# Mask rows made on chip from nine columns, the first pair's loads issued first, and a new engine and order table: attention, gated convolution and spatial gating on one core

## The chip, the cores and the metric

One core of a Trainium2 chip runs the whole program. The metric is device time in microseconds (us), and lower is better. A run's time is that of the whole execution; the profile's span, from the first to the last instruction, is about two us shorter. A matmul on TensorE (PE in the rows) takes its stationary operand by a weight load (PEld); VectorE is DVE, ScalarE is ACT, GpSimd is POOL, SyncE is SP.

## The reference

Three layers follow one another on B = 4 sequences of S = 576 positions.

```python
scores = scale * np.matmul(q, k.transpose(0, 1, 3, 2))      # 8 heads of 64
mask = block_i >= block_j                                   # blocks of 64 positions
scores = np.where(mask, scores, -1000000000.0)
attn = np.exp(scores - np.max(scores, axis=-1, keepdims=True))
attn = attn / (np.sum(attn, axis=-1, keepdims=True) + 1e-09)
x = np.matmul(attn, v)                                      # heads side by side: 512 wide
...
h = np.maximum(x @ w_in, 0.0)                               # 512 -> 1024
conv_out = sum over k of conv_w[k] * hp[:, k:k + S, :]      # 3 taps along the sequence
x = h * sigmoid(conv_out) @ w_out                           # 1024 -> 512
...
h = np.maximum(x @ w_in, 0.0); u, v = halves of h
v_n = (v - mean) / np.sqrt(var + 1e-06)
out = (u * (w_spatial @ v_n + b_spatial)) @ w_out
```

## The kernel before, in words

The 32 heads are handled as 16 pairs; a pair's two heads lie in the two halves of the 128 partitions. Nearly every float32 product is made of three matmuls on parts: a rounded part (`..._h`, type fp32r) and the rest of it (`..._l`), so each operand is rounded once (a copy to fp32r) and subtracted once. Two weights arrive as 64-bit words and are put together by a few integer operations (`words_to_f32`, `split64`).

A pair goes through these steps. `load_pairs` brings K and Q (`raw`), `prep_pair` rounds them to `kp` and `qp` and the last 64 queries to `qlast` (lines 685, 686 and 666: ACT, DVE or POOL). Five `x` steps on PE find the largest score of each 64-query block: four of them multiply (line 916 in row halves, line 655 for the step with `qlast`, which writes the two `mo` banks or one `st` tile), DVE reduces them (lines 921, 950, 956), `max_up` joins them (line 969), and the fifth transposes the maxima (line 978). They are copied to `mt` and sent by DMA into two rows of `mq` (line 990). The `s` steps multiply K by Q (line 1034 or 1042) and then add mask and maximum in one more product, `mk` by `mq` (line 1046); ACT takes the exponential (line 1055). The `v` step multiplies by V and by ones (line 663), and `norm_a` divides by the sums. Four pairs give a batch's `x`, on which the `m` steps (lines 655 with `x,w1i` and `g,w1o`) do the second layer; each tile of it passes through ACT and DVE (lines 1205 to 1215) and is rounded into `g`. The `p` steps do the third layer.

The mask works through `mk` and `mq`, 128 partitions by 576 columns each. Row 0 (and 64) of `mk` is -1 and meets the maximum in `mq`; rows 1 to 4 of `mk` are 1 in the odd 64-column blocks, and meet rows of `mq` that are -2^30 in the even blocks. Before the change DVE zeroes `mk` and the three `mq` (line 1361), and POOL issues eight DMAs that bring the rows from a constant in memory (line 1332).

The order of all engines is fixed by tables. `SEQ` is a string with one letter for each step of PE (`x`, `y` for the `qlast` step into `mo`, `s`, `v`, `m`, `p`; a capital takes the other ring of PSUM banks; `f` is a filler: `FILL_N` matmuls on a tile of ones, kept for PE to have work). `ORDER` lists for DVE, ACT, POOL and SP which task gives the next instruction, `BIND` which buffer each task takes, and `ENG` which engine does each rounding or subtraction (one letter for each: `K`, `Q` and `QE` are `kp`, `qp` and the two `qlast` parts, `GH` the rounding of `g`). While the program is built, the class `Order` replays a plan of time with a cost for each instruction, and emits the instructions in the tables' order. An engine runs its list strictly in order: an instruction that waits holds all behind it.

At the start, 16 spinning matmuls on the tile of ones (line 1344) keep PE at work until the first loads land. `first` holds SP for `HEAD`; then SP issues the first pair's load in two parts (256 and 320 columns, line 832), with the load of the convolution's weights (`cwr`, line 1377) between them, then pair 1 (line 841) and the rest. A filler before the change writes columns 290 to 512 of both `mo` banks without taking them:

```python
def fill(got):
    o = od_mo[0]
    for _ in range(FILL_N):
        if od.tile:
            for e in range(2):
                r = slice(64 * e, 64 * e + 64)
                nc.tensor.matmul(od_mo[e][:, 290:512], full[r, 0:128], full[r], start=True, stop=True)
```

Of the kernel before, what the change touches and what calls it, by code (L numbers as in the profile page):

```python
# [26 lines left out]
KROWS = 69  # L27
# [1803 lines left out]
```

## Time and profile before

| | us |
|---|---|
| median of 3 runs (lowest, highest) | 598.27 (597.57, 598.81) |
| the profiled execution | 597.48 |
| its span | 595.4 |
| PE busy in the span | 576.0 (97%) |
| DVE busy | 448.4 (75%) |
| ACT busy | 247.6 (42%) |
| POOL busy | 166.0 (28%) |

The sum of any term is made against the profiled execution (597.48, 0.79 under the median). Busy time of PE includes overlapping matmuls counted once. A mean over the span hides that the engines that set the pace change: so the rows further down go by stretches.

### The profile page before, as it was taken

Reading aid. Unit: us, or ns where it says so; the run is one execution under the profiler, and the core shown is the slowest. Engines: PE = TensorE matmul, PEld = TensorE weight load, DVE = VectorE, ACT = ScalarE, POOL = GpSimd, SP = SyncE. Lnnn points to the kernel's source line nnn. Section 1 sums busy time; section 2 is a strip of 40 time slices with the busy share of each in tenths; the row PEclk is TensorE's granted clock in tenths of the full one; section 3 lists DMA queues with packets and bytes.
Section 4 is the critical chain, followed back from the end, with each engine's and each line's share of the span. In section 5 each row is a group of like instructions: output and inputs, shape, how many; then the busy total and the mean of one; then the engine's idle time right before and its main releaser. Section 6 shows DMA issues by size and latency. Waiting matters only on the chain.

```text
span 595.4 us, 11879 instructions
## 1 busy us (share of the span) xinstructions
PE 576.0 (97%) x4606; PEld 514.9 (86%) x4606; DVE 448.4 (75%) x985; ACT 247.6 (42%) x527; POOL 166.0 (28%) x206
## 2 busy tenths in 40 slices
PE   7899998999999999999999999999999999999997
PEld 5666678789988888789988999999899989998997
DVE  6899999988577879858558699866897456456557
ACT  3354666645355525617454565533253023103101
POOL 3346653312233353221500033333311111112121
PEclk9999999999999999999999999999999999999999
DMA  6557542231212334021111736334602500150002
GB/s 188 189 163 229 186 153 94 83 97 68 65 37 84 103 125 144 22 84 61 41 63 58 246 106 193 102 107 138 222 0 90 168 21 0 51 177 14 21 30 91
DMA packets 43542, 61.22 MB, mean 103 GB/s; under 512 B 8949, under 2 KB 34293, under 8 KB 43486
## 3 DMA queue, kind: packets, MB, share of 16 engines
q1 hardware_dynamic: 43226, 60.37, 31.7%
q8 instruction: 36, 0.59, 0.4%
q14 instruction: 20, 0.16, 0.1%
q0 software_dynamic: 256, 0.09, 0.1%
q10 hardware_dynamic: 4, 0.00, 0.0%
HBM read 46.08 MB, written 14.23 MB: 101 GB/s over the span
## 4 chain that ended last, share of the span: by engine, by line
PE 70%; DVE 15%; POOL 4%; ACT 3%; issue 3%; DMA 2%; SPq 0%; DVEq 0%; ACTq 0%; POOLq 0%
PE mo L655 42%; PE s L655 9%; PE st L663 7%; PE st L1042 4%; PE st L1034 2%; PE st L916 2%; DVE cc L1211 2%; PE st L1046 2%; DVE mx L921 1%; DVE w_f L780 1%; DVE g L669 1%; PE st L655 1%; POOL g L666 1%; DMA w_raw<-in_w2o_dram 1%; DMA raw<-in_kq_dram 1%
## 5 line engine op out<-in xcount | busy, mean ns | idle before, releaser
L655 PE MATMUL mo<-x,w1i_h 128*128 128x290 f32 x504 | 106.9, 300 | 0.0
L655 PE MATMUL mo<-g,w1o_h 128*128 128x288 f32 x464 | 98.2, 298 | 0.3 <-DVE y L1248 0.3
L655 PEld LDWEIGHTS mo<-x,w1i_h 128*128 128x128 f32 x504 | 82.8, 188 | 2.0 <-issue 1.3
L655 PEld LDWEIGHTS mo<-g,w1o_h 128*128 128x128 f32 x464 | 76.2, 189 | 3.4 <-issue 2.1
L655 PE MATMUL mo<-x,w1i_l 128*128 128x290 f32 x252 | 75.0, 298 | 0.0
L1211 DVE SCALAR_TENSOR_TENSOR cc<-h,cwt,cc 128x288 f32<-128x288 f32 x128 | 67.1, 539 | 7.6 <-ACT cc L1208 6.6
L655 PE MATMUL mo<-g,w1o_l 128*128 128x288 f32 x232 | 68.5, 295 | 0.0
L1055 ACT ACTIVATE e<-st 128x1024 f32<-128x1024 f32 (+2 forms) x64 | 52.9, 836 | 26.4 <-PE st L1046 24.9
L655 PE MATMUL mo<-x,w2i_h 128*128 128x288 f32 x256 | 52.3, 296 | 0.1
L666 POOL TENSOR_SCALAR g<-ga 128x288 fp32r<-128x288 f32 x40 | 20.2, 512 | 108.8 <-DVE ga L1548 59.7
L921 DVE TENSOR_REDUCE mx<-st 128x2 f32<-128x128 f32 (+2 forms) x64 | 42.4, 680 | 8.5 <-PE st L916 8.5
L655 PEld LDWEIGHTS mo<-x,w1i_l 128*128 128x128 f32 x252 | 47.5, 188 | 0.0
L666 POOL TENSOR_SCALAR g<-cc 128x288 fp32r<-128x288 f32 x23 | 14.9, 651 | 115.8 <-DVE cc L1215 113.0
L663 PE MATMUL st<-e,v 128*64 128x448 f32 (+4 forms) x384 | 46.7, 392 | 0.1
L663 PEld LDWEIGHTS st<-e,v 128*64 128x64 f32 x384 | 25.0, 137 | 22.6 <-issue 16.8
L655 PEld LDWEIGHTS mo<-g,w1o_l 128*128 128x128 f32 x232 | 43.5, 188 | 0.1
L655 PEld LDWEIGHTS mo<-x,w2i_h 128*128 128x128 f32 x256 | 41.4, 188 | 1.0 <-ACT u L1522 0.8
L655 PE MATMUL mo<-ws_h,vnh 128*128 128x288 f32 x135 | 39.6, 297 | 1.1 <-DVE ga L1548 1.1
L655 PE MATMUL s<-w2i_h,x 128*128 128x512 f32 x128 | 39.5, 390 | 0.0
L1046 PE MATMUL st<-mq,mk 64*128 64x320 f32 (+1 forms) x192 | 37.9, 394 | 0.0
L655 PE MATMUL mo<-x,w2i_l 128*128 128x288 f32 x128 | 37.7, 294 | 0.0
L1208 ACT ACTIVATE cc<-h,cwt 128x288 f32<-128x288 f32 x64 | 33.8, 533 | 9.1 <-DVE g L669 8.0
(203 smaller groups left out, 1396.5 us busy)
## 6 DMA issues: line engine op xcount, KB each, us to landing
x2d<-y SPq DMA_DIRECT2D x32, 288.0 KB
x<-x2d SPq DMA_DIRECT2D x16, 576.0 KB
raw<-in_kq_dram SPq DMA_DIRECT2D x15, 576.0 KB
v<-in_vt_dram SPq DMA_DIRECT2D x16, 320.0 KB
rb<-rd SPq DMA_DIRECT2D x32, 144.0 KB
out_dram<-o SPq DMA_DIRECT2D x32, 144.0 KB
x<-in_w2i_dram SPq DMA_DIRECT2D x8, 512.0 KB
w_raw<-in_w1i_dram SPq DMA_DIRECT2D x4, 512.0 KB
```

Source lines behind the costliest of these rows:

```text
L655: nc.tensor.matmul(o, w, x, start=start, stop=stop)
L663: nc.tensor.matmul(o[row:row + m], w, x, start=start, stop=stop)
L666: nc.gpsimd.tensor_scalar(o, i, 1.0, 0.0, ALU.mult, ALU.add)
L669: nc.vector.tensor_tensor(o, a, b, ALU.subtract)
L916: nc.tensor.matmul(st[:, e, o:o + n], qp[r, 128 * c:128 * c + 128], kp[r, 0:n], start=True, stop=True)
L921: return ("DVE", t_dve(2 * i.shape[-1] * (i.shape[2] if len(i.shape) == 4 else 1)), lambda: nc.vector.tensor_reduce(o, i, AX.X, ALU.max), ...
L1034: nc.tensor.matmul(out, keys(RAW[p][:, 0, :], r), RAW[p][r, 1, q0:q0 + nq], start=True, stop=False)
L1042: nc.tensor.matmul(st[:, e, o:o + nq], keys(kx, slice(64 * e, 64 * e + 64)), qx[e], start=j == 0, stop=False)
L1046: nc.tensor.matmul(st[:, e, o:o + nq], keys(mk, r), q[r, q0:q0 + nq], start=False, stop=True)
L1055: yield ("ACT", t_act(2 * n), lambda: nc.scalar.activation(ex[:, :, e0:e0 + n], st[:, :, 0:n], ACTF.Exp, scale=0.125), 0, 0)
L1208: yield ("ACT", t_act(HT, False, 1), lambda: nc.scalar.activation(cc, h[:, o:o + HT], ACTF.Copy, scale=cwt[:, c, 1:2]), 0, P_G)
L1211: yield ("DVE", t_dve(HT, ptr=1), lambda: nc.vector.scalar_tensor_tensor(cc, h[:, o + e:o + e + HT], cwt[:, c, j:j + 1], cc, ALU.mult, ALU ...
```

## The change

- The mask rows are made on chip. One DMA on ACT's queue brings `sel`, nine columns by 128 partitions. ACT makes `mk` in six instructions (`start3`: ones times a column plus a column), POOL makes the first `mq` in four and copies it to the other two (`start`). DVE zeroes only the first `mq`; POOL's eight DMAs are gone. The maxima of any pair now wait for `mqs` as well.
- Both parts of the first pair's load are issued first, then the first block of `w1i`, `cwr`, and pair 1.
- A filler takes one `mo` bank, writes its columns 0 to 222, and gives it back. In a stretch of row-half matmuls it uses 64 rows and one matmul in place of two side by side; `SEQ` has two `f` in place of three.
- The plan counts POOL's roundings on the port that DVE and POOL share, with another cost for them (`t_round`), and a few more DVE instructions. `SEQ`, `ORDER`, `BIND` and `ENG` are new. In all, POOL has 185 listed rows for 206, ACT 556 for 524, DVE 957 for 949: kp and qp roundings on POOL go from 17 to 7, on ACT (whole tiles) from 9 to 17.

```diff
-                for e in range(2):
-                    q.dma_start(out=t[64 * e:64 * e + 5], in_=kc[c])
...
     def start():
-        yield ("POOL", 1.9, consts([(mk, 0)], nc.gpsimd))
+        yield ("wait", ("head",))
+        for c in range(4):
+            yield ("POOL", 0.4 + 0.5 * (c == 0), lambda: nc.gpsimd.tensor_scalar(
+                mq[0][:, 128 * c:128 * c + 64], raw(full[:, 0:64]), sel[:, 5 + c:6 + c], None, ALU.mult), 0, 0, True)
+        for t in mq[1:]:
+            yield ("POOL", t_round(S), lambda: pool_round(t, raw(mq[0])), 0, 0, True)
+        yield ("mark", ("mqs",))
+
+    def start3():
+        yield ("wait", ("head",))
+        for c in range(4):
+            yield ("ACT", 0.25 + 0.5 * (c == 0), lambda: nc.scalar.activation(
+                mk[:, 128 * c + 64:128 * c + 128], raw(full[:, 0:64]), ACTF.Identity, bias=sel[:, 4:5], scale=sel[:, c:c + 1]), 0, 0)
...
+    def fill_step():
+        def fn(got):
+            o = got["mo"][0]
+            for _ in range(FILL_N):
+                mm(o[:, 0:222], full[0:64 if od.tile else 128, 0:128], full[0:64 if od.tile else 128], True, True)
+            slot.append(o)
+        slot = []
+        return dict(needs=[], rings=[("mo", 1)], fn=fn, frees=lambda: [("mo", slot)], tile=od.tile)
...
     def zeros():
-        spin(od_mo[0])
+        nc.scalar.dma_start(out=sel, in_=kc)
+        spin()
         nc.vector.memset(eps, 1e-6)
-        for t in [mk] + mq:
-            nc.vector.memset(raw(t), 0.0)
+        nc.vector.memset(raw(mq[0]), 0.0)
...
-            self.port = start + dur
+            self.port = start + dur - 0.13 * (eng == "POOL")
...
-            return ("POOL", t_round(n), fn, 0, prio, False)
+            return ("POOL", t_round(n), fn, 0, prio, True)
...
-    "K": "APPPPDPPPAAAAPPPP",
+    "K": "DAPADAAPAAPAAAADP",
```

Where the instructions moved, at three places.

SP, the start of its list (`raw` is a pair's K and Q, `w_raw` and `x` hold blocks of `w1i`). Before:

```order
L832 DMA raw<-in_kq_dram 128x2x256
L1377 DMA cwr<-in_cw_dram 128x48
L832 DMA raw<-in_kq_dram 128x2x320
L841 DMA raw<-in_kq_dram 128x1152
L1390 DMA ident<-in_cst_dram 128x128
```

Now:

```order
L830 DMA raw<-in_kq_dram 128x2x256
L830 DMA raw<-in_kq_dram 128x2x320
L790 DMA w_raw_143<-in_w1i_dram 128x4x256
L1384 DMA cwr<-in_cw_dram 128x48
L839 DMA raw<-in_kq_dram 128x1152
L1397 DMA ident<-in_cst_dram 128x128
```

The second part stands next to the first; pair 1 stands behind a block of `w1i`.

PE and DVE around the fillers of pair 1 (the `mo<-kp,qlast` matmuls are its `y` step, `mxl` the reductions of that step, `mo<-full` the fillers). PE before:

```order
L655 MATMUL mo_109<-kp_155,qlast_152 128x288
L655 MATMUL mo_110<-kp_155,qlast_152 128x288
L916 MATMUL st_111<-kp_155,qp_156 128x128 x2
L916 MATMUL st_111<-kp_155,qp_156 128x256 x2
L1352 MATMUL mo_109<-full 128x222
L1352 MATMUL mo_110<-full 128x222
```

PE now:

```order
L653 MATMUL mo_110<-kp_156,qlast_153 128x288
L653 MATMUL mo_111<-kp_156,qlast_153 128x288
L914 MATMUL st_113<-kp_156,qp_157 128x128 x2
L914 MATMUL st_113<-kp_156,qp_157 128x256 x2
L653 MATMUL mo_110<-full 128x222 x2
L1033 MATMUL st_114<-raw 128x256 x2
L653 MATMUL mo_110<-full 128x222 x2
L1045 MATMUL st_112<-mq_149,mk 128x320 x2
```

DVE before:

```order
L969 SCALAR_TENSOR_TENSOR mx<-mxu,lim,mx 128x8
L686 CAST qp_156<-raw 128x576
L778 SCALAR_TENSOR_TENSOR cwr<-cwr 128x24
L686 CAST qlast_152<-raw 64x64
L772 TENSOR_SCALAR w_raw_142<-w_raw_142 128x512
L778 SCALAR_TENSOR_TENSOR w_raw_142<-w_raw_142 128x512
L956 TENSOR_REDUCE mxl<-mo_109 128x1
L956 TENSOR_REDUCE mxl<-mo_110 128x1
```

DVE now:

```order
L967 SCALAR_TENSOR_TENSOR mx<-mxu,lim,mx 128x8
L684 CAST qlast_153<-raw 64x64
L684 CAST qp_157<-raw 128x576
L776 SCALAR_TENSOR_TENSOR w_raw_143<-w_raw_143 128x512
L770 TENSOR_SCALAR cwr<-cwr 128x24
L954 TENSOR_REDUCE mxl<-mo_110 128x1
L778 SCALAR_TENSOR_TENSOR w_f_139<-w_f_139,w_raw_143 128x512
L919 TENSOR_REDUCE mx<-st_113 128x2
L954 TENSOR_REDUCE mxl<-mo_111 128x1
```

The fillers follow the first `mxl` instead of being followed by it, and only one bank is concerned.

POOL at the preparation of pair 14 (`kp`, `qp`, `qlast` in a row). Before:

```order
L666 TENSOR_SCALAR g_119<-cc_133 128x288
L666 TENSOR_SCALAR kp_155<-raw 128x576
L666 TENSOR_SCALAR qp_156<-raw 128x576
L666 TENSOR_SCALAR qlast_152<-raw 64x64
L692 TENSOR_TENSOR x_2817<-xp_131,x_2817 128x576
```

Now, on ACT (and `qp` on DVE, the other half of `qlast` on POOL):

```order
L1054 ACTIVATE e_130<-st_113 128x2x512
L683 ACTIVATE kp_156<-raw 128x576
L1054 ACTIVATE e_130<-st_112 128x2x512
L1212 ACTIVATE cc_134<-cc_134 128x288
L1204 ACTIVATE h_145<-mo_110 128x290
L683 ACTIVATE qlast_153<-raw 64x64
```

Of three instructions in a row on POOL, one is left there.

## Rows read from the trace of the kernel before

**Rows 1.** Windows: busy us of each engine by stage, granted clock, DMA share.

```profile
core 0: us, PE busy (x) PEld busy (x) DVE busy (x) ACT busy (x) POOL busy (x), PEclk, DMA share, GB/s
...
30.00:120.00 90.00, 83.61 (x886) 64.48 (x882) 87.13 (x188) 53.23 (x99) 45.77 (x47) 1.00 0.47 149
120.00:265.00 145.00, 143.15 (x1242) 123.47 (x1243) 112.04 (x231) 68.00 (x139) 43.27 (x47) 1.00 0.27 85
```

**Rows 2.** Chain that ended last, first 26 us: start us, us, what.

```profile
2.09 4.75 DMA raw<-in_kq_dram
...
7.69 0.70 PE st L916 x2
```

**Rows 3.** Timeline of SP: start us, us, line, operation, out<-in.

```profile
0.75 0.66 SPq L832 DMA_DIRECT2D raw<-in_kq_dram  x1
1.47 0.58 SPq L1377 DMA_DIRECT2D cwr<-in_cw_dram  x1
2.09 0.56 SPq L832 DMA_DIRECT2D raw<-in_kq_dram  x1
```

**Rows 4.** Timeline of DVE from 14 us; brackets: idle before, releaser.

```profile
14.43 0.46 DVE L956 TENSOR_REDUCE mxl<-mo 128x1 f32<-128x288 f32 x1 [0.94 <-PE mo L1352]
15.75 0.46 DVE L956 TENSOR_REDUCE mxl<-mo 128x1 f32<-128x288 f32 x1 [0.86 <-PE mo L1352]
```

**Rows 5.** Timeline of PE, 1 to 30 us.

```profile
1.16 3.75 PE L1344 MATMUL mo<-full 128*128 128x222 f32 x16 [1.16 <-DVE eps L1359]
...
15.50 0.72 PE L1046 MATMUL st<-mq,mk 64*128 64x320 f32 x4
17.65 1.12 PE L916 MATMUL st<-kp,qp 64*128 64x384 f32 x4 [1.43 <-DVE mxu L921]
...
20.93 1.42 PE L1034 MATMUL st<-raw 64*128 64x320 f32 x4
...
23.37 0.51 PE L655 MATMUL mo<-kp,qlast 128*128 128x288 f32 x2
...
29.30 0.81 PE L1034 MATMUL st<-raw 64*128 64x320 f32 x4
```

**Rows 6.** Groups by form, DVE: xcount, busy us, mean ns, idle before.

```profile
L1361 DVE MEMSET mq<- 128x576 f32 x3 | 1.6, 538 | 0.2
L669 DVE TENSOR_TENSOR raw<-raw,kp 128x576 fp32r<-128x576 f32 x7 | 5.2, 748 | 1.1 <-PE st L1034 1.0
L669 DVE TENSOR_TENSOR w1o_l<-w_f,w1o_h 128x512 fp32r<-128x512 f32 x7 | 5.9, 845 | 0.0
L686 DVE CAST g<-cc 128x288 fp32r<-128x288 f32 x9 | 2.7, 304 | 0.2
L686 DVE CAST x<-xp 128x576 fp32r<-128x576 f32 x2 | 0.9, 460 | 0.1
```

**Rows 7.** Groups by form, ACT.

```profile
L685 ACT ACTIVATE kp<-raw 128x576 fp32r<-128x576 f32 x4 | 2.7, 672 | 0.0
L685 ACT ACTIVATE w1i_h<-w_f 128x512 fp32r<-128x512 f32 x2 | 1.2, 622 | 1.3 <-DVE w_f L780 1.3
L685 ACT ACTIVATE qlast<-raw 64x64 fp32r<-64x64 f32 x10 | 2.5, 251 | 2.5 <-DMA raw<-in_kq_dram 2.3
```

**Rows 8.** Waits, whole span: engine, line, waited for, us in total, times, longest.

```profile
ACT e L1055 <- PE st L1046: 24.9, 26, 4.6
...
PE st L1042 <- ACT e L1055: 1.2, 2, 0.7
PE st L916 <- ACT e L1055: 0.4, 2, 0.2
PE st L1034 <- ACT e L1055: 0.3, 1, 0.3
```

**Rows 9.** Timeline of POOL and PE, pair 14.

```profile
236.21 2.19 POOL L666 TENSOR_SCALAR qlast<-raw 64x64 fp32r<-64x64 f32 x1
...
238.45 0.53 PE L655 MATMUL st<-kp,qlast 128*128 128x288 f32 x2 [1.12 <-POOL qlast L666]
```

More of the change, by code (lines that the diff above doesn't have):

```diff
@@ L26 @@
 VO = 384
-KROWS = 69
 NQ = 3
@@ L230 @@
     ),
[12 rows of a table removed]
-    ),
     "e0": (
@@ L590, in run, with dma @@
             fn()
-def dma(od, size, fn, prio=0, issue=0.48, hot=False):
+def dma(od, size, fn, prio=0, issue=0.48, hot=False, key=None):
     if size > 65536:
@@ L597, in dma @@
     yield ("SP", issue, fn, 0, prio)
+    if key:
+        yield ("mark", key)
     if hot:
@@ L613, in t_round @@
 def t_round(n):
-    return 0.317 + n * 0.00056
+    return 0.146 + n * 0.00084
 def t_ptt(n):
@@ L702, in attn_moe_moe2_kernel @@
     lim = const.tile([128, 1], F32, name="lim")
+    sel = const.tile([128, 9], F32, name="sel")
     ones = const.tile([128, 32], F32, name="ones")
@@ L745, in bank @@
         return t[:, 0, :] if len(t.shape) == 3 else t
-    od_mo = list(od.slots["mo"])
     full = att.tile([128, 222], F32R, name="full")
@@ L818, in load_pairs @@
     def load_pairs():
-        yield ("wait", ("head",))
         for p in range(NPAIR):
+            yield ("wait", ("head",) if p else ("head0",))
             late = None
@@ L826, in load_pairs @@
             HELD[p] = [slot]
-            od.spawn(prep_pair(p, RAW[p], slot, late), "att")
-            if p == 0:
-                yield ("sleep", 0.01)
+            od.spawn(prep_pair(p, RAW[p], slot, late), "att", 0.0, f"pp{p}")
     def first_load(o, i, part):
-        yield from dma(od, o.shape[1] * o.shape[2] * 512, lambda: nc.sync.dma_start(out=o, in_=i), -1)
+        if part:
+            yield ("wait", ("head1",))
+        yield from dma(od, o.shape[1] * o.shape[2] * 512, lambda: nc.sync.dma_start(out=o, in_=i), -1, key=(("head", "head1")[part == 0],))
         yield ("mark", ("raw", 0, part))
@@ L986, in task @@
                 m = MROW[p] = yield ("take", "mq")
+                yield ("wait", ("mqs",))
                 def row(i, q):
@@ L1290, in head @@
         if c == "f":
-            return dict(needs=[], rings=[], fn=fill, tile=od.tile)
+            return fill_step()
         if c in "xy":
@@ L1325, in attn_moe_moe2_kernel, with ones_by @@
     od.pick = pick
-    def consts(tiles, q):
-        def ld():
-            for t, c in tiles:
-                for e in range(2):
-                    q.dma_start(out=t[64 * e:64 * e + 5], in_=kc[c])
-        return ld
-    def start():
-        yield ("POOL", 1.9, consts([(mk, 0)], nc.gpsimd))
+    def ones_by(n):
+        return raw(full[:, 0:64 * n]).rearrange("p (i x) -> p i x", x=64)
+    def start():
+        yield ("wait", ("head",))
[5 more added lines that the diff above has]
+        yield ("mark", ("mqs",))
@@ new lines, in start3 @@
+    def start3():
[3 more added lines that the diff above has]
+                mk[:, 128 * c + 64:128 * c + 128], raw(full[:, 0:64]), ACTF.Identity, bias=sel[:, 4:5], scale=sel[:, c:c + 1]), 0, 0)
+        even = mk[:, 0:384].rearrange("p (i x) -> p i x", x=128)[:, :, 0:64], mk[:, 384:S].rearrange("p (i x) -> p i x", x=64)[:, 0:3:2, :]
+        for o, n in zip(even, (3, 2)):
+            yield ("ACT", 0.33, lambda: nc.scalar.activation(o, ones_by(n), ACTF.Identity, bias=sel[:, 4:5], scale=0.0), 0, 0)
@@ L1337, in start, with spin @@
         yield ("mark", ("mk",))
-        yield ("POOL", 3.2, consts([(t, 1) for t in mq], nc.gpsimd))
-    def spin(o):
+    def spin():
         nc.vector.memset(raw(full), 1.0)
         for _ in range(SPIN):
-            nc.tensor.matmul(o[:, 290:512], full[:, 0:128], full, start=True, stop=True)
-    def fill(got):
-        o = od_mo[0]
-        for _ in range(FILL_N):
-            if od.tile:
-                for e in range(2):
-                    r = slice(64 * e, 64 * e + 64)
-                    nc.tensor.matmul(od_mo[e][:, 290:512], full[r, 0:128], full[r], start=True, stop=True)
-                od.cost += 0.113
-            else:
-                mm(o[:, 290:512], full[:, 0:128], full, True, True)
+            nc.tensor.matmul(od.slots["mo"][0][:, 0:222], full[:, 0:128], full, start=True, stop=True)
@@ L1484, in task @@
                 if c < 4:
-                    yield ("POOL", t_round(512), lambda: pool_round(vnh[:, c], v), 0, 1)
-                    yield ("DVE", t_dve(512), lambda: sub(vnl[:, c], v, raw(vnh[:, c])), 0, 1)
+                    yield ("POOL", t_round(512), lambda: pool_round(vnh[:, c], v), 0, 1, True)
+                    yield ("DVE", t_dve(512), lambda: sub(vnl[:, c], v, raw(vnh[:, c])), 0, 1, True)
                     yield ("free", "vf", v)
@@ L1494, in task @@
                     ta, tb = vnh[:, 4 + e], vnl[:, 4 + e]
-                    yield ("POOL", t_round(512), lambda: pool_round(ta[own], v[own]), 0, 1)
-                    yield ("DVE", t_dve(512), lambda: sub(ta[far], v[own], raw(ta[own])), 0, 1)
+                    yield ("POOL", t_round(512), lambda: pool_round(ta[own], v[own]), 0, 1, True)
+                    yield ("DVE", t_dve(512), lambda: sub(ta[far], v[own], raw(ta[own])), 0, 1, True)
                     yield ("ACT", t_act(512, False), lambda: nc.scalar.activation(tb[0:64], v[own], ACTF.Copy), 0, 1)
@@ L1594, in parts @@
         else:
-            yield ("POOL", t_round(HT), lambda: pool_round(g[:, 0], src), 0, 1)
+            yield ("POOL", t_round(HT), lambda: pool_round(g[:, 0], src), 0, 1, True)
         yield ("DVE", t_dve(HT), lambda: sub(g[:, 1], src, raw(g[:, 0])), 0, 0, True)
@@ L1709, in ws_unit @@
             yield ("DVE", t_dve(S), lambda: sub(ws_l[96:97, c], r[64:65], raw(ws_l[64:65, c])), 0, 1)
-        yield ("DVE", t_dve(S), lambda: sub(ws_l[0:k, c], r[0:k], raw(ws_h[0:k, c])), 0, 1)
+        yield ("DVE", t_dve(S), lambda: sub(ws_l[0:k, c], r[0:k], raw(ws_h[0:k, c])), 0, 1, True)
         yield ("free", "wr", slot)
@@ L1797 @@
     cst = _np.eye(128, dtype=_np.float32)
-    kc = _np.zeros((2, KROWS - 64, S), dtype=_np.float32)
-    kc[0, 0] = -1.0
-    for c in range(4):
-        kc[0, 1 + c, 128 * c + 64:128 * c + 128] = 1.0
-        kc[1, 1 + c, 128 * c:128 * c + 64] = NEG
+    kc = _np.zeros((128, 9), dtype=_np.float32)
+    for e in (0, 64):
+        kc[e, 4] = -1.0
+        for c in range(4):
+            kc[e + 1 + c, c] = 1.0
+            kc[e + 1 + c, 5 + c] = NEG
     arrs = {
```

75 lines of the change are left out of this document (37 added, 38 removed), and 302 rows, old and new, of tables (BIND, ORDER).

## The prediction

> **What bounds the kernel now.** I read the windows by stage first, since the whole span's 97% for PE says nothing of where time could be won. From 120 to 265 us PE is busy 143.2 of 145 us: there only PE's own work or one of its few waits can give anything. From 30 to 120 us PE is busy 83.6 of 90, but DVE 87.1 of 90, so DVE sets the pace there, with ACT at 53.2 and POOL at 45.8 [rows 1]. What is left is the first 30 us. So I read the chain of waits there: the second part of the first pair's load is issued at 2.09 us and takes 4.75 us to land, and PE can multiply with it at 7.69 [rows 2]. Then the timelines of SP, DVE and PE over that stretch, to see what each of them waits for [rows 3 to 5]. Last, PE's waits, of which the longest late one stands at 238 us [rows 9].
>
> **Part by part.**
>
> Loads. The second part is issued at 2.09 because `cwr` stands ahead of it [rows 3]. In the new list it stands right behind the first, whose issue ends at 0.75 + 0.66 = 1.41; so it goes out at about 1.47, where `cwr` does now: 0.62 earlier. Everything up to the first mask product hangs on it [rows 2]. What moves behind it is pair 1 (past a block of `w1i` and `cwr`); pair 1 is multiplied only after the first pair's maxima (DVE reduces its `qlast` step from 14.43 on [rows 4]), and that is its cover. Without the cover the first exponentials are not touched, only pair 1's. I take **-0.62**; bounds 0 (the transfer is held up by the block behind it) and -0.62.
>
> Fillers. DVE's two reductions of pair 1's `qlast` step each wait for a filler, 0.94 and 0.86 us [rows 4]: the filler writes other columns of the same bank, and stands behind the product and ahead of its reduction. PE then waits 1.43 us for DVE before the next step at 17.65 [rows 5]. In the new order the fillers take the bank after the first reduction has freed it, so DVE waits for no filler. PE can gain at most its own 1.43, as the step ahead, the mask products at 15.50 [rows 5], need their row of maxima by DMA anyway. Against that DVE has one more long instruction (joining a block of `w1i`) between the two reductions. Bounds 0 and -1.43; I take **-1.0**, nearer the wait that the rows show than nothing.
>
> Masks. Three zeroings leave DVE, 3 x 0.538 = 1.6 us [rows 6], but at a time when all wait for the first load: nothing. Eight DMA issues leave POOL. Six instructions come to ACT: four of 64 columns, about 0.25 each by the 64-column rounding, and two longer ones of at most 0.67 each by the 576-column one [rows 7], 2.3 us in all; about as much comes to POOL. Two of ACT's stand ahead of its part of `qp`, 0.5 us, and wait for the nine columns. If these land late, the first product does too, but the gap of PE ahead of the second part at 7.69 [rows 2] takes that up. **0**; bounds 0 and +0.5.
>
> DVE's list. Up to the 17th gate instruction (line 1215, well past the stretch that DVE paces), eight instructions go: two subtractions into `raw` at 0.75, one `w1o_l` at 0.845, five others that I take at the middling 0.46 of an `x` rounding [rows 6], 4.65 in all. Ten come: three `g` roundings at 0.304, two of `x` at 0.46 [rows 6], five others at 0.46, 4.13 in all. Net **-0.5**. Bounds 0 (DVE's waits take it) and -2.1 (with the 1.6 of the zeroings).
>
> ACT's list. Ahead of the first tile of the second layer ACT gets five more `kp` roundings at 0.672, three `w1i_h` at 0.622 [rows 7], and five of like size (0.65): 3.36 + 1.87 + 3.25 = 8.5 us. With 53.2 of 90 us busy [rows 1] that makes about 69%. PE's waits for ACT's exponentials are 1.2 + 0.4 + 0.3 = 1.9 us [rows 8]; raised by 8.5 / 53.2 they grow by **+0.3**. Bounds 0 and, if each of these instructions holds up an exponential that PE waits for, +8.5.
>
> Pair 14. POOL rounds a 64-column piece of `qlast` in 2.19 us where ACT's mean is 0.251, and PE waits 1.12 us for it [rows 7, 9]. In the new lists ACT does `kp`, DVE `qp`, and POOL only one half of `qlast`. That half can be as slow, but comes sooner, with no `kp` and `qp` ahead of it. Bounds -1.12 and 0; I take **-0.7**.
>
> Fillers as work, the plan's port and costs: they change the tables alone, and PE's list is otherwise the same to within six matmuls of 222 columns, four of them side by side with another. 0.
>
> Sum: -0.62 - 1.0 - 0.5 + 0.3 - 0.7 = -2.5. Of the profiled execution, 597.48, that leaves 594.96; the median of the runs shown is 0.79 higher, so the forecast against the median is **595.7 us**.
>
> **A rule weighed: the clock.** The granted clock stands at 1.00 in every window [rows 1], yet the rows say otherwise for the beginning. Four matmuls of 320 columns take 1.42 us at 20.93 and 0.81 at 29.30, and the pair of 288 columns at 23.37 takes 0.51 [rows 5]: before about 23 us PE ran at the lower of its two levels, 1.2 GHz, and rose to 2.4 GHz after having worked without a gap from 17.65 on. The spinning matmuls from 1.16 to 4.91 [rows 5] had not been enough. My sum lets the rise move with the work: it comes earlier by what the work does. The Trainium skill, "TensorE: Matmul & The Clock Gate", section "What's actually happening", says that the array starts throttled, that activity releases it, and that the point of release differs between runs of the same kernel. By that rule the rise need not follow the work, and either half of the dense stretch could go to one level or the other; this is the first rival.
>
> **The rivals.**
>
> *The clock rises elsewhere.* From 17.65 to about 23.4, 5.75 us of PE's work run at half rate and lie on the chain. If the gap of 1.43 us ahead of it closes and the rise comes at the start of it, half is saved: -2.9 more, 592.8 us. For it: PE's work from 13 us on would be without a gap. Against it: the fillers are half the matmuls that they were, and 3.75 us of spinning did not raise it. As far the other way, a rise 5.75 us of work later, it gives 595.7 + 2.9 = 598.6, no change. Chance 0.17 for the early rise.
>
> *The stalls are only traded.* The mask row's DMA, not the filler, decides the product at 15.50, so -1.0 goes; POOL's half of `qlast` at pair 14 is as slow as now, so -0.7 goes; DVE's -0.5 is lost in new waits. What remains is -0.62 + 0.3: 598.27 - 0.3 = 598.0. For it: DVE's list has the same length, and PE is 98% busy after 120 us. With the late clock: chance 0.20.
>
> *ACT's queue becomes what PE waits for.* ACT runs its list strictly in order. The `kp` roundings that it takes over wait for a pair's load, and an exponential stands behind each. Then a score tile is not freed, the next `x` step of PE has no place, and DVE, which paces this stretch, gets nothing to reduce. At the full price of 8.5 in place of 0.3 the time is 595.7 + 8.2 = 603.9. It decides when more than 2.5 + 0.3 + 1.2 = 4.0 us of the 8.5 reach PE, about half. For it: 69% of an in-order engine in a stretch where every engine feeds another. Against it: ACT's exponentials wait 24.9 us for PE, PE 1.9 for them [rows 8]. Chance 0.18.
>
> That the change doesn't do what it says I leave out: the lists show the fillers, loads and masks moved.
>
> **How the numbers follow.** A measurement of this kernel can tell about 0.2%, 1.2 us, from no change (the three runs lie 1.24 apart). The forecast has 0.45, the early clock 0.17, both over 1.2 us faster: 0.62. No change has 0.20, slower 0.18. The range goes from 591.0, the early clock with DVE's larger bound (592.8 - 1.6 = 591.2), up to 599.5, which takes in the traded stalls, the late clock and the beginning of ACT's rival. Below lie some 0.04, above about 0.14 of ACT's 0.18.
>
> **What would show it.** The second part's load issued near 1.5 us and PE's 384-column product near 7.1. No wait of DVE's `mxl` for a filler, and PE's next such product for pair 1 near 16 us in place of 17.65. The pair of 288-column matmuls of pair 2 before 22 us. No wait of PE for POOL's `qlast` over 0.4 us near pair 14. From 30 to 120 us DVE still at 95% or more, with as much of PE's work done some 2 us sooner. I am wrong if PE's waits for ACT's `e` or for ACT's `kp` pass 4 us, if the first product with `kp` comes later than 5.8 us because of the nine columns, or if PE's busy share from 120 to 265 us falls.

## The result, and the profile after

| | before | the change |
|---|---|---|
| median, us (lowest to highest, 4 runs each) | 598.02 (597.57 to 598.81) | 587.22 (586.77 to 587.94) |
| ratio to before, 95% interval | | 0.9819 (0.9802 to 0.9836) |
| the profiled execution, its span | 597.48, 595.4 | 587.56, 585.8 |
| busy: PE, DVE, ACT, POOL | 576.0, 448.4, 247.6, 166.0 | 573.6, 438.0, 260.7, 152.1 |

The change is 10.8 us faster. The forecast was 595.7, 2.3 under the median of this comparison, with a range from 591.0 to 599.5: the sign was right, the size was not, and the measured time lies below the range.

To see where the time came from I took the same matmul in both traces (same operands, same number of its kind) at nine places, and subtracted its times. "Forecast" is the sum of the prediction's terms that belong to a stretch; places are those of the trace after.

| stretch (us of the trace after) | shorter by | forecast |
|---|---|---|
| 0 to 24.9 (head) | 2.24 | 1.62 (loads, fillers) |
| 24.9 to 43.0 | 0.00 | |
| 43.0 to 84.9 | 0.82 | 0.2 (DVE's list, ACT's list) |
| 84.9 to 126.1 | 2.50 | (the same) |
| 126.1 to 199.8 | 0.07 | |
| 199.8 to 242.1 (pair 14) | 1.81 | 0.7 |
| 242.1 to 345.0 | -0.16 | |
| 345.0 to 452.0 (third layer's preparation) | 2.68 | 0 (tables) |
| to the end | -0.02 | |

The sum is 9.94, the difference of the two profiled executions (597.48 - 587.56 = 9.92).

The windows after, which answer to [rows 1] (columns: stretch, its length, busy us and instructions of PE, PE's weight loads, DVE, ACT, POOL, then the granted clock, DMA share, GB/s):

```profile
30.00:120.00 90.00, 85.47 (x904) 67.20 (x901) 84.44 (x197) 58.00 (x108) 34.54 (x32) 1.00 0.47 151
120.00:265.00 145.00, 144.91 (x1278) 126.17 (x1277) 110.83 (x227) 73.42 (x150) 40.99 (x42) 1.00 0.27 86
```

From 30 to 120 us DVE does nine instructions more than before and is busy 2.7 us less; POOL does 15 fewer and is busy 11.2 us less. From 120 to 265 PE is idle for 0.09 us in place of 1.85. The gain from 85 on is plainest in windows of their own, before and after (same columns):

```profile
43.00:85.00 42.00, 38.77 (x471) 28.15 (x471) 40.65 (x91) 24.23 (x38) 24.88 (x22) 1.00 0.64 200
85.00:126.00 41.00, 38.46 (x337) 33.27 (x326) 38.89 (x83) 24.13 (x55) 16.58 (x18) 1.00 0.21 72
```

```profile
43.00:85.00 42.00, 39.51 (x476) 28.79 (x475) 39.33 (x88) 28.39 (x48) 23.37 (x19) 1.00 0.64 197
85.00:126.00 41.00, 40.09 (x345) 35.31 (x344) 38.40 (x89) 25.45 (x54) 8.37 (x10) 1.00 0.22 77
```

From 85 to 126 POOL's time is halved, and DVE does six instructions more in less time.

The head, PE's timeline after (start, us, line, operation; in brackets the idle time before and its releaser), to be held against [rows 5]:

```profile
6.28 1.11 PE L914 MATMUL st<-kp,qp 64*128 64x384 f32 x4 [0.65 <-POOL kp L664]
...
14.88 0.68 PE L914 MATMUL st<-kp,qp 64*128 64x384 f32 x2
...
18.73 1.42 PE L1033 MATMUL st<-raw 64*128 64x320 f32 x4
...
21.11 0.51 PE L653 MATMUL mo<-kp,qlast 128*128 128x288 f32 x2
```

The product with the second part of the load starts at 6.28 (7.69 before), the first product of pair 1 behind the stall at 14.88 (17.65), and the first 288-column pair at 0.51 us, thus at 2.4 GHz, at 21.11 (23.37).

### The profile page after: what moved, and what is told of

Read it like the earlier page. It is cut to its first block, busy times and chain, and to the rows that moved or that the text cites. A ratio compares the mean times of both kernels' runs of the same rounds, so it can differ in the third digit from the quotient of the medians.

```text
span 585.8 us, 11845 instructions
## 1 busy us (share of the span) xinstructions
PE 573.6 (98%) x4600; PEld 514.9 (88%) x4600; DVE 438.0 (75%) x980; ACT 260.7 (45%) x554; POOL 152.1 (26%) x185
## 4 chain that ended last, share of the span: by engine, by line
PE 89%; DVE 6%; DMA 2%; issue 1%; ACT 1%; SPq 0%; DVEq 0%; POOL 0%
PE mo L653 55%; PE s L653 14%; PE st L661 8%; PE st L1041 4%; PE st L1033 2%; PE st L914 2%; PE st L1045 2%; DVE mx L919 1%; PE st L653 1%; DVE w_f L778 1%; DMA rb<-rd 1%; ACT e L1054 1%; DMA raw<-in_kq_dram 1%; DVE xp L1172 1%; DVE mxu L919 0%
## 5 line engine op out<-in xcount | busy, mean ns | idle before, releaser
L1210 DVE SCALAR_TENSOR_TENSOR cc<-h,cwt,cc 128x288 f32<-128x288 f32 x128 | 65.9, 532 | 8.2 <-ACT cc L1207 7.2
L919 DVE TENSOR_REDUCE mx<-st 128x2 f32<-128x128 f32 (+3 forms) x64 | 42.8, 682 | 8.9 <-PE st L914 8.5
L664 POOL TENSOR_SCALAR g<-ga 128x288 fp32r<-128x288 f32 x40 | 18.9, 478 | 114.5 <-DVE ga L1556 54.3
L1212 ACT ACTIVATE cc<-cc 128x288 f32<-128x288 f32 x64 | 27.6, 439 | 23.1 <-DVE cc L1210 22.9
L1204 ACT ACTIVATE h<-mo 128x290 f32<-128x290 f32 x63 | 25.7, 409 | 23.6 <-PE mo L653 16.7
## 6 DMA issues: line engine op xcount, KB each, us to landing
x<-x2d SPq DMA_DIRECT2D x16, 576.0 KB
raw<-in_kq_dram SPq DMA_DIRECT2D x15, 576.0 KB
```

The costliest lines, as they stand in the source:

```text
L664: nc.gpsimd.tensor_scalar(o, i, 1.0, 0.0, ALU.mult, ALU.add)
L919: return ("DVE", t_dve(2 * i.shape[-1] * (i.shape[2] if len(i.shape) == 4 else 1)), lambda: nc.vector.tensor_reduce(o, i, AX.X, ALU.max), ...
L1204: yield ("ACT", t_act(290), lambda: nc.scalar.activation(h[:, 1:291], ps[:, 0:290], ACTF.Relu), 0, 0)
L1210: yield ("DVE", t_dve(HT, ptr=1), lambda: nc.vector.scalar_tensor_tensor(cc, h[:, o + e:o + e + HT], cwt[:, c, j:j + 1], cc, ALU.mult, ALU ...
L1212: yield ("ACT", t_act(HT, False), lambda: nc.scalar.activation(cc, cc, ACTF.Tanh, scale=0.5), 0, P_G)
```

## The experiments

Each run's arrivals at the same places, against the trace of the change or of before, in us (plus is later or longer). "Time" is a median where more than one run was timed; e5, e6, e7, e10, e11, e13, e14 and e18 were timed once. These runs were made on four other chips, on which the kernel before has medians from 596.19 to 596.85, so times of different chips are compared by their ratio to before where there is one.

| run | time | to 43 us | 43 to 126 | 200 to 242 | 345 to 452 |
|---|---|---|---|---|---|
| against the change: e1 loads back | 587.79 | +0.18 | +0.21 | 0 | -0.07 |
| e2 old fillers | 587.76 | +0.76 | -0.59 | 0 | -0.04 |
| e3 no fillers | 585.87 | -1.12 | +0.03 | 0 | -0.10 |
| e4 head alone | 595.65 | -1.25 | +5.32 | +1.81 | +2.67 |
| e5 15 roundings | 589.10 | -1.56 | +3.23 | -0.01 | -0.04 |
| e6 30 roundings | 596.73 | -1.54 | +10.70 | 0 | -0.07 |
| e7 15 zeroings | 587.50 | -0.09 | +0.22 | 0 | -0.08 |
| e8 old engines back | 593.19 | -1.14 | +4.81 | -0.01 | -0.07 |
| e10 pair 14 back | 587.27 | -0.88 | +0.52 | +0.12 | -0.04 |
| e12 ten more to ACT | 589.82 | -1.51 | +3.60 | -0.01 | -0.09 |
| e15 the change again | 587.17 | -0.20 | +0.96 | 0 | -0.13 |
| e16 no fillers again | 586.41 | -0.92 | +2.50 | 0 | -0.06 |
| e17 fillers near 70 us | 586.00 | -1.85 | +0.04 | -0.01 | -0.11 |
| e18 old tables from 345 | 592.30 | -0.50 | +0.70 | -0.01 | +4.84 |
| against before: e9 new engines | 599.71 | -1.09 | +4.66 | -0.02 | -0.20 |
| e11 `ga` first | 595.80 | -0.55 | -0.30 | 0 | -0.88 |
| e13 13 to ACT | 594.53 | -0.63 | -1.76 | 0 | -0.31 |
| e14 pair 14 first | 595.71 | -1.04 | +0.09 | -0.74 | +0.05 |

First a caution on the column "to 43 us". e5, e7, e10 and e15 have the same program as the change up to some 35 us, and still differ by up to 1.56 us there; so do the kernels of before (0 to -1.04). TensorE's clock differs there between executions (further down). A difference in the head under 1.5 us between two profiles is therefore no finding by itself. Over several profiles the head's gain stands: the matmul at 24.9 us comes between 25.9 and 27.2 in the five with the head of before, and between 23.5 and 25.0 in seven with that of the change (itself, e5, e6, e7, e10, e15, e18), 1.9 earlier on average.

From 43 to 126 us executions of one program differ as well, with the clock at 1.00: e10, e15 and e18 have the program of the change there and come 0.52, 0.96 and 0.70 later. In e15 the 175 instructions that DVE starts in that stretch take 90.61 us, in the change 89.66; half of the 0.95 is one joining of maxima (`mx<-mxu,lim,mx`) that takes 0.60 us beside a rounding of POOL's and 0.12 without one.

### The head: e1 to e4

e1 puts `cwr` back between the two parts of the first load (here and below, a piece of a table's string).

```diff
-first_load0 first_load1 split64 start2
+first_load0 start2 first_load1 split64
```

> The changed kernel with the convolution's weights loaded between the two parts of the first pair's load again, as before. Theory A (each gain of the first 25 us is kept to the end): the second part is issued some 0.6 us later, the first product of 384 columns comes 0.6 later (6.9 in place of 6.28 us), and the end too: 587.2 + 0.6 = 587.8. Theory B (the stretch that DVE paces swallows what the head gains): the product is 0.6 later, the end is not: 587.2.

The product of 384 columns came at 7.45, 1.17 later (5.66 to 6.28 in the seven profiles with the head of the change), but by 24.9 us only 0.31 was left of it, and the median is 587.79. The order of the loads is worth some tenths of a us; whether 0.3 or 0.6 can't be told here.

e2 lets the fillers write columns 290 to 512 again, without a bank of their own.

> The changed kernel with the fillers of before: they write columns 290 to 512 of both banks without taking them. Theory A: DVE's two reductions of pair 1's last block wait for a filler again (0.9 us each in the profile of before), PE's step with x7, at 14.88 now, comes about 1.4 later, and the end too: 588.6. Theory B: that wait is hidden by the row of maxima, which comes by DMA: x7 and the end are as now, 587.2.

DVE's second reduction waits for a filler again (DVE's timeline of e2):

```profile
14.97 0.46 DVE L953 TENSOR_REDUCE mxl<-mo 128x1 f32<-128x288 f32 x1 [1.34 <-PE mo L1360]
```

Pair 1's product behind it comes at 16.62 in place of 14.88, and 1.2 us are lost by 85 us; from there to 126 us 1.01 come back, and 0.10 is left at the end. What comes back is one instruction of DVE's, the joining of a block of weights. POOL and DVE in the change, then in e2:

```profile
83.27 1.29 POOL L690 TENSOR_TENSOR w1o_l<-w_f,w1o_h 128x512 fp32r<-128x512 f32 x1 [2.42 <-ACT w1o_h L683]
83.32 1.78 DVE L778 SCALAR_TENSOR_TENSOR w_f<-w_f,x 128x512 uint32<-128x512 uint32 x1
```

```profile
84.50 1.81 POOL L689 TENSOR_TENSOR w1o_l<-w_f,w1o_h 128x512 fp32r<-128x512 f32 x1 [2.48 <-ACT w1o_h L682]
84.47 0.69 DVE L777 SCALAR_TENSOR_TENSOR w_f<-w_f,x 128x512 uint32<-128x512 uint32 x1
```

In the change POOL starts 0.05 us earlier and DVE's instruction takes 1.78 us (1.66 to 1.81 in all the other runs made from the change, e4 with its old tables apart); in e2 DVE starts 0.03 earlier and takes 0.69. The wait for the filler was real. How much of it would reach the end without that accident is open: the medians (587.76 and 587.22) don't tell it, as e2's own runs lie 3.7 us apart.

e3 takes the fillers out of `SEQ` altogether.

> The changed kernel without any filler. If the fillers hold up the granted clock, its rise (21 us now) comes later, by up to 5 us of PE's work at half rate: up to 2.5 us more, 589.7. If they are work and nothing else, PE saves four to six matmuls in a stretch where it waits anyway: 587.2, and no more than 0.4 less.

585.87: the fillers don't hold up the clock in the head (the 384-column product of pair 1 stands at 14.96, and 288 columns take 0.54 us from 20.68 on). Its profile is 1.12 us ahead of the change's at 43 us and 1.13 at the end, so a lead from the head isn't always lost in the stretch that DVE paces. How much the fillers cost is taken up with e16.

e4 joins the change's tables up to 22 us to those of before.

> The changed kernel with the tables of the change up to 22 us of the plan and those of before (order, engines, buffers) for all that comes later; masks, loads and fillers as in the change. Theory A: what is gained by 22 us, 2.2 to 2.8 us, is kept and nothing else comes: 598.0 - 2.3 = 595.7. Theory B (swallowed): 598.0. Theory C (an earlier head lets the later lists run as well as they do in the change): 587 to 589.

595.65, ratio 0.9977 (0.9957 to 0.9997). PE is 3.5 us ahead of before at 43 us, and 1.5 at 126. The 2 us are lost by 55 us, and the largest piece is one integer operation of DVE's on `w_raw`: 1.91 us beside a subtraction of POOL's, 0.67 in before. That the old tables always take such a lead back is not shown: e11 and e14, which have them too, are 0.56 and 1.04 ahead at 43 us and 0.85 and 0.95 at 126. About 1 us of the head's gain reaches the end. So the rest, 8 to 9 us, hangs on the tables behind the head.

### Work on POOL: e5 to e9, e12, e13

e5 and e6 add roundings on POOL to the change, which nobody waits for (e6 has `range(2)`); e7 adds zeroings in the same places.

```diff
+    def extra():
+        yield ("wait", ("mk",))
+        for _ in range(1):
+            yield ("POOL", 0.6, lambda: pool_round(dump, raw(mk)), 0, 0, False)
```

> The changed kernel with 15 more roundings of 128x576 on POOL, of the mask into a tile that nobody reads, put into the gaps of POOL's list from 35 to 125 us; POOL's busy time of that stretch is then about that of before (34.5 + 15 x 0.75 = 45.8 us). Theory P (DVE is slowed by POOL's work on SBUF, and DVE sets the pace): DVE's instructions that lie beside POOL's take longer, by 0.2 to 0.25 us for each us of overlap, so 11 us more of POOL cost DVE 2.2 to 2.8 us and PE about as much by 125 us: 589.5 to 590. Theory O (the gain is in the order of the lists alone): POOL is idle two thirds of the time and nobody waits for the extra roundings: 587.2 to 587.6.

> The same with two roundings in each of the 15 gaps, 30 in all. Theory P: twice the price of 15, so 4.4 to 5.6 us: 592. Theory O: up to 1 us, where a pair of them holds up a real one of POOL's: 588.

> 15 zeroings of a 128x576 tile on POOL at the places of the 15 roundings: as much of POOL's time or less, but with one stream (it writes and does not read). If what slows DVE is POOL's reading and writing of SBUF, it costs less than the roundings, about half: 588.4. If it is any work on POOL: as the 15 roundings. If POOL's list itself (the real roundings behind the extra ones start late) is the cause: as the 15 roundings too.

The windows of e5, then of e7:

```profile
30.00:120.00 90.00, 83.96 (x877) 65.94 (x874) 85.42 (x190) 56.73 (x105) 45.70 (x45) 0.98 0.46 146
43.00:85.00 42.00, 39.14 (x463) 29.05 (x460) 38.50 (x84) 26.48 (x46) 25.35 (x25) 0.96 0.62 196
85.00:126.00 41.00, 38.88 (x335) 33.88 (x334) 39.47 (x88) 25.50 (x56) 12.95 (x16) 1.00 0.20 70
```

```profile
30.00:120.00 90.00, 85.41 (x903) 67.06 (x900) 85.43 (x197) 57.88 (x107) 42.27 (x47) 1.00 0.47 151
```

With 15 roundings POOL is as busy as before (45.70; [rows 1] has 45.77), and 3.23 us are lost. Up to 1.7 of them can belong to TensorE's clock, which was granted at 0.65 and 0.78 in two stretches of 3 us ((0.35 + 0.22) x 3). What remains at least, 1.5 us, is 0.1 for each rounding, and alone it would not stand clear of the 0.96 by which e15 differs.

DVE's own rows settle it, as they don't follow that clock: in e16, where it falls to 0.50 (further down), DVE's instructions of the stretch take 89.81 us, in e3, the same program without the fall, 89.66. DVE's list is the same in the change and in e5, e6 and e7, so the 175 instructions that it starts from 43 to 126 us in the change can be compared one by one. They take 89.66 us in the change, 92.94 with 15 roundings on POOL (3.28 more, 0.22 for each), 95.07 with 30 (5.41 more) and 89.65 with 15 zeroings. With 15 zeroings POOL runs as many instructions (47) for nearly as long, and nothing is lost: it isn't POOL's time, and not its list. What differs is that a rounding also reads SBUF. 30 roundings cost PE 10.70, of which up to 5.1 can be stretches at half clock. The Trainium skill, "SBUF — State Buffer", section "SBUF: two separate sides", says that DVE and GpSimd share one pair of ports, that an instruction holds it whole, and that a DVE instruction with two SBUF inputs meets only a GpSimd one that reads SBUF. e5 and e7 agree with that, by 3.28 us against none.

What it does to a DVE instruction stands in the trace of before. DVE's timeline:

```profile
95.09 0.91 DVE L669 TENSOR_TENSOR g<-cc,g 128x288 fp32r<-128x288 f32 x1
...
101.62 0.46 DVE L669 TENSOR_TENSOR g<-cc,g 128x288 fp32r<-128x288 f32 x1
...
102.43 0.46 DVE L1215 SCALAR_TENSOR_TENSOR cc<-cc,h 128x288 f32<-128x288 f32 x1
...
103.83 0.90 DVE L1215 SCALAR_TENSOR_TENSOR cc<-cc,h 128x288 f32<-128x288 f32 x1
```

and POOL's:

```profile
94.83 0.87 POOL L666 TENSOR_SCALAR qp<-raw 128x576 fp32r<-128x576 f32 x1
...
103.57 1.75 POOL L769 TENSOR_SCALAR w_raw<-w_raw 128x512 f32<-128x512 f32 x1
```

The same subtraction takes 0.46 us alone and 0.91 beside POOL's rounding; the same gate product 0.46 alone and 0.90 beside POOL's operation on `w_raw`.

e13 takes load off POOL in the kernel before, and changes nothing else: 13 of its roundings go to ACT, for instance

```diff
-    "K": "APPPPDPPPAAAAPPPP",
+    "K": "APPAPDAPAAAAAPPPP",
```

> The kernel before with 13 roundings of 22 to 125 us moved from POOL to ACT, the same 13 that the change moves from POOL to ACT there, all else as before. Theory P (less work on POOL beside DVE is the gain): at 0.1 to 0.2 us for each rounding taken off, 1.3 to 2.6 us less from 43 to 126 us. Theory O (an engine's list and its places only pay together): no gain there, or a loss of some us, since ACT's list holds exponentials behind roundings that wait for a load.

1.76 us less from 43 to 126 us, 0.135 for each rounding, inside what theory P expected. DVE's list is that of before, and the same 172 instructions take 88.61 us in place of 91.44, 2.83 less or again 0.22 for each rounding. In e11 and e14, where this stretch is as in before, they take 90.71 and 91.61, and PE comes 0.30 earlier and 0.09 later. (The other 0.9 of its 2.65 at the end lie mostly in the head.) So about half of the 3.32 us that the change gains there is had by relieving POOL alone, in the old order. In the change itself, 171 of DVE's instructions of that stretch of before, matched by kind and count, take 88.45 us in place of 90.75.

e8 gives the change the engines of before for 61 instructions of that stretch; e9 gives before the engines of the change for the same 61.

> The changed kernel with the engine of before for each of the 61 roundings, subtractions and copies that the change gave to another engine between 22 and 125 us of the plan; each stands in its new list at the place in time at which it stood in the old one, all else in the order of the change. POOL gets back 14, ACT loses 10, DVE 4. Theory P: DVE's instructions are slowed as before (3.8 us more beside POOL, less some 1.7 for four instructions that leave it), 2 to 4 us lost by 125 us: 589 to 591. Theory O: the order is what gained, and is kept: 587.2 to 588.

> The kernel before, with the engine of the change for each of those 61 roundings, subtractions and copies of 22 to 125 us; each stands in its new list at the place in time at which it stood in the old one, all else (order, head, fillers, masks) as before. Theory P (the choice of engine alone relieves DVE): from 43 to 126 us PE gains the 3.3 us that the change gained there, or somewhat less since the order was not fitted to it: 598.0 - 3 = 595.0. Theory O (engines and order only pay together, since an in-order list needs the places that go with its engines): 597 to 600.

e8 loses 4.81 us from 43 to 126, with the clock at 1.00 throughout, more than the change had gained: with the old engines the order of the change is worse than the old one. e9 loses 4.66, of which up to 3.4 can be half clock from 78 to 87 us; the rest, at least 1.3, is still a loss, and its six runs are slower than before (ratio 1.0048, 1.0031 to 1.0066). So the other half of the gain belongs to the engines and the order together, and neither has it alone. I did not divide it further.

e12 goes on in the same direction: no fillers, and ten more roundings from POOL to ACT.

> The changed kernel without fillers, and with ten more roundings of 30 to 126 us moved from POOL to ACT (five of w1i or w1o, four of kp or qp, one of g), about 9 us of POOL's time. Theory P: at 0.2 to 0.25 us of DVE's time for each us of overlap, 1.8 to 2.2 us less than without fillers alone: 583.9. Rival (ACT's list is the next bound: PE's waits for exponentials, 0.8 and 0.4 us now, grow): 586 to 588.

589.82. POOL is relieved once more, but PE waits more for exponentials: its waits from 43 to 126 us in e12, then in the change (line, what for, us in total, times, longest; one more wait of 0.8 us stands in each):

```profile
PE st L913 <- ACT e L1053: 1.3, 3, 0.5
```

```profile
PE st L914 <- ACT e L1054: 0.4, 2, 0.2
```

The clock fell as well (0.70, 0.50 and 0.66 in three stretches of 3 us from 72 on, up to 3.4 us of the 3.60). DVE's 175 instructions take 89.12 us, 0.54 less than in e3 (89.66), while PE's waits for exponentials in that stretch are 1.1 us longer than there (2.1 and 1.0). So even at full clock a gain is not to be seen. The prediction's third rival, ACT's list, begins to show just beyond the change; its price can't be told from this run, for the clock.

### Pair 14: e10 and e14

e10 puts pair 14's `kp`, `qp` and `qlast` back on POOL, in the change.

> The changed kernel with the preparation of pair 14 on the engines of before: kp, qp and one half of qlast in a row on POOL. If that row is the cause of PE's stop near 238 us of before: POOL's qlast takes about 2 us beside DVE again, PE waits for it 1.1 us or more, and the stretch from 200 to 242 us is 1.4 to 1.8 us longer: 588.6 to 589. If it was the place in POOL's list that delayed it and not the row: no wait of PE, 587.2.

It costs nothing (0.12): POOL's `qlast` takes 0.33 us there. Not the engine, then. In the trace of before POOL stood for 11.69 us in front of a rounding of `g`, with pair 14 behind it:

```profile
232.95 1.13 POOL L666 TENSOR_SCALAR g<-cc 128x288 fp32r<-128x288 f32 x1 [11.69 <-DVE cc L1215]
234.05 0.87 POOL L666 TENSOR_SCALAR kp<-raw 128x576 fp32r<-128x576 f32 x1
```

e14 puts that `g` behind the three, in the kernel before.

```diff
-m52 one1400 one1401 ends14
+one1400 one1401 ends14 m52
```

> The kernel before with pair 14's kp, qp and half of qlast ahead of one rounding of g on POOL and not behind it (POOL stood 11.7 us in front of that g, until DVE had made it). Theory: PE's stop of 1.39 us near 238 us is the place in the list: it goes, and the stretch from 200 to 242 us is 1.2 to 1.4 us shorter. Rival: DVE keeps POOL's qlast slow, whatever its place (2.19 us for a 64x64 rounding), so PE still waits 0.5 us or more.

POOL in e14:

```profile
231.21 0.81 POOL L666 TENSOR_SCALAR kp<-raw 128x576 fp32r<-128x576 f32 x1 [10.87 <-PE st L1046]
231.98 0.88 POOL L666 TENSOR_SCALAR qp<-raw 128x576 fp32r<-128x576 f32 x1
232.94 0.96 POOL L666 TENSOR_SCALAR qlast<-raw 64x64 fp32r<-64x64 f32 x1
```

PE's wait for `qlast` is gone, and 0.74 of the 1.81 us with it; a new wait of 0.5 us for DVE's `mx` takes part of the place:

```profile
PE st L663 <- DVE mx L950: 0.5, 1, 0.5
```

The place in POOL's list was the cause of the stop, and DVE's list stood close behind it. What else makes up the 1.81 was not tried.

### The third layer's preparation: e11 and e18

In before DVE waits 2.71 us for ACT to make `w_f`, with a product `ga` behind it that PE needs:

```profile
418.25 0.43 DVE L772 TENSOR_SCALAR w_raw<-w_raw 128x512 uint32<-128x512 uint32 x1 [2.71 <-ACT w_f L764]
418.72 0.69 DVE L778 SCALAR_TENSOR_TENSOR w_raw<-w_raw 128x512 uint32<-128x512 uint32 x1
419.33 0.45 DVE L1548 TENSOR_TENSOR ga<-u,mo 128x288 f32<-128x288 f32 x1
```

```diff
-p14 w2o_f320*2 p15 w2o_f322
+p14 p15 w2o_f320*2 w2o_f322
```

> The kernel before with one instruction of DVE's list moved: the product ga of the third spatial step stands ahead of the two integer operations on a block of w2o and not behind them (in before DVE waited 2.71 us there for ACT's w_f, with ga ready behind it, and PE then 1.1 us for ga). Theory: PE's wait at 420 us goes, 1.1 to 1.4 us less from 390 to 452 us: 596.8. Rival: the integer operations come later by it, so the weights w2o are late in their turn, and PE waits there instead: 598.

```profile
416.32 0.45 DVE L1548 TENSOR_TENSOR ga<-u,mo 128x288 f32<-128x288 f32 x1 [1.39 <-PE mo L655]
417.19 0.43 DVE L772 TENSOR_SCALAR w_raw<-w_raw 128x512 uint32<-128x512 uint32 x1 [0.42 <-ACT w_f L764]
```

In e11 `ga` is made as soon as PE has its input, DVE's idle time falls to 0.42, and 0.88 us are gained (e9, e13 and e14 differ from before by up to 0.31 in that stretch): a third of what the change gains from 345 to 452 us, by one instruction moved.

> The change with its own tables up to 345 us of the plan and those of before for all that comes later. If the order of the third layer's preparation in those tables is the gain of 345 to 452 us: 2.7 us back, 589.9, with PE's waits near 385, 420 and 447 us of before in their places again. Rival (the gain is that all data are there sooner, whatever the order): 587.2.

592.30: the old tables from 345 us on cost 2.17 us from 390 to 452, what the change had gained there (2.12), and 2.67 from 345 to 390, where the change had gained 0.56; the rest of that is a wait of 1.9 us for DVE's `y` at the place where the two tables are joined. The gain of this stretch is the tables.

### A version that beats both? e15 to e17

> The change itself once more, as a measure for the next kernel on the same chip: 587.2, ratio to before 0.982.

> The change without fillers once more, beside the change on the same chip. If the saving of 1.1 us that its profile showed (all of it by 43 us) is no accident of the clock: 586.0, 1.0 to 1.4 less than the change. If it is one: the same as the change within 0.4.

The change 587.17, without fillers 586.41, on one chip; the ratios to before are 0.9837 (0.9811 to 0.9864) and 0.9833 (0.9808 to 0.9858). No difference is shown. The profile of e16 takes 2.71 us more from 43 to 85 us than that of e3, which is the same program. Windows of e16, then of e3:

```profile
69.00:72.00 3.00, 1.79 (x19) 1.28 (x19) 2.96 (x9) 1.91 (x4) 1.86 (x2) 0.96 0.29 96
72.00:75.00 3.00, 3.00 (x19) 2.54 (x19) 2.92 (x6) 1.96 (x4) 1.15 (x1) 0.50 0.84 242
75.00:78.00 3.00, 3.00 (x26) 2.78 (x26) 0.03 (x1) 2.16 (x3) 1.31 (x2) 0.50 0.39 141
```

```profile
69.00:72.00 3.00, 1.79 (x20) 1.29 (x17) 2.96 (x9) 2.13 (x4) 1.65 (x2) 1.00 0.32 105
72.00:75.00 3.00, 2.92 (x38) 2.58 (x37) 2.70 (x6) 2.98 (x5) 1.28 (x2) 1.00 0.81 266
```

In both PE is busy 1.79 of the 3 us from 69 on. In e16 the granted clock then falls to 0.50, and PE does 19 matmuls in the next 3 us; in e3 it stays at 1.00, and PE does 38. e17 puts the fillers there, at the two places where PE waits:

```diff
 L1045 MATMUL st_112<-mq_151,mk 128x320 x2
+L653 MATMUL mo_110<-full 128x222 x4
 L1041 MATMUL st_112<-qp_155,kp_154 128x256 x2
```

> The change with its two fillers moved from the first pair's steps to the gaps of PE near 70 us (ahead of the second score step of the pair that waits 0.8 us for an exponential, and ahead of the transposition that waits 0.41 for DVE), four matmuls each in place of two. If work in that gap keeps the clock at 1.00 there: all runs near 585.9, the best of those without fillers, ratio to before 0.981 or less. Rival: the clock falls there whatever PE does in the gap, or the fillers hold up the steps behind them: 586.5 to 589, as without fillers.

```profile
69.00:72.00 3.00, 2.64 (x25) 2.12 (x24) 2.96 (x7) 2.82 (x6) 0.92 (x1) 1.00 0.50 182
```

PE is busy 2.64 of these 3 us, the clock stays at 1.00, and no time is lost from 43 to 126 (+0.04). Five runs lie between 585.29 and 586.76, median 586.00. That beats before (ratio 0.9822, 0.9807 to 0.9837). That it beats the change is not shown, for the change's own ratios are 0.9819 and, in e15, 0.9837; nor can one profile show that the fillers kept the clock.

## Why the prediction was wrong

The sum was 2.5 us; the two profiled executions lie 9.9 apart. Of the 7.4 us between, 3.1 arise from 43 to 126 us, 2.7 in the third layer's preparation, 1.1 at pair 14 and 0.6 in the head.

- **Loads, -0.62.** Both parts are issued by 2.05, as forecast, and the 384-column product comes at 6.28, earlier than the 7.1 that was named. Their worth is uncertain: in e1 1.17 at the product, 0.3 left at 24.9.
- **Fillers, -1.0.** The mechanism was right (no wait for a filler, 14.88 in place of 17.65, back with e2), and so was the size at 24.9 (0.76). What of it reaches the end is open: 0.10 in e2, where one DVE instruction happened to start ahead of POOL's. The sum added a gain ahead of the stretch that DVE paces as if it passed through; in e3 it did, in e4 only in part.
- **Masks, 0.** Right: the first product with `kp` starts at 4.84, as in before (4.85).
- **DVE's list, -0.5, bounds 0 and -2.1: the step that failed most.** It counted DVE's own instructions, each at the mean of its group in the trace of before. Those means held POOL's interference; the term "Eight instructions go ... ten come" did not ask what ran beside them. That POOL loses 21 instructions stood in the order, and its 45.77 us in [rows 1], but no term priced them. In the change DVE does the same instructions of 43 to 126 us in 2.3 us less. The sign that the prediction set, DVE at 95% or more from 30 to 120 us, was missed: 84.44 of 90 is 93.8%. By e13, 13 roundings less give 1.76 us, and the engines and order together 3.32.
- **ACT's list, +0.3, bound +8.5.** Small, as forecast, with the sign the other way: PE's waits for exponentials are 1.6 us in place of 1.9. In e12 they are 2.8.
- **Pair 14, -0.7, bounds 0 and -1.12.** Right in sign; the stretch gave 1.81. The step named the wrong cause: "no `kp` and `qp` ahead of it" costs nothing to undo (e10); the `g` in front of all three did it (e14).
- **"Fillers as work, the plan's port and costs: they change the tables alone ... 0": the second step that failed.** Behind 265 us no list was compared. The tables gave 2.68 us there (e18), a third of it from one row (e11).
- **Rivals.** The early clock was a real possibility of the head, as a difference between executions and not between kernels. Stalls were traded only for part of the head's gain (e4). ACT's queue did not bind in the change.

## What to carry to other kernels

Where DVE sets the pace, price a neighbour on its port by taking work off that neighbour (here 0.22 us of DVE's time for each rounding added or moved, and 0.14 of the program's for each one moved), and don't take a group's mean as DVE's own cost. To tell interference from order, compare the same instructions of the paced engine one by one in two traces; here their sum did not follow TensorE's clock (e16 and e3). In an engine that runs strictly in order, look for the longest idle time and read what is ready behind it: two such rows gave 0.74 and 0.88 us with one entry moved each. And compare two traces by the same matmul along the whole program before believing in a cause, and two executions of one program before believing in a difference: here they lie up to 1 us apart in one stretch with the clock at 1.00.

## What the runs showed of the hardware

- A two-input DVE instruction that meets one of POOL's that reads SBUF takes longer: 0.91 us in place of 0.46, 0.60 in place of 0.12, 1.78 in place of 0.69. In the last case a start 0.05 us earlier or 0.03 later on POOL's side decided which of the two was the slow one (the change and e2). 15 zeroings of the same size as the roundings cost DVE nothing (e7). In the other direction POOL's 64x64 rounding took 2.19 us among DVE's work [rows 9], and 0.33 in e10.
- TensorE's clock differs between executions of one program. In the change the 384-column product took 1.11 us at 6.28, thus at the lower level of 1.2 GHz; in e5, the same program up to some 35 us, it took 0.67, and the granted clock then fell (0.65 on average from 10 to 15 us). By the Trainium skill, "TensorE: Matmul & The Clock Gate", section "What's actually happening", the point of release varies from run to run; these traces agree, by up to 1.56 us at 43 us.
- It also fell in the middle of the work: to 0.50 from 72 to 78 us in e16, though no wait of PE just before it was longer than 0.80 us, and not in e3, the same program. e16 takes 2.7 us more from 43 to 85 us.
